# ScalarE's queue order, whole-row state copies and a halved last transfer in a kernel of two sequence layers

## The chip, the cores and the metric

The kernel runs on one core of one Trainium2 chip. The metric is the device time of one execution in microseconds; less is better. The kernel before takes 144.13 us, the median of three runs (144.0 to 144.6).

## The reference

Two independent layers on sequences of 2048 tokens with 448 features, their outputs side by side.

```
# A: a diagonal complex state space layer (448 states)
Lam_bar = exp(dt * Lam);  Bu = x @ B_bar.T
h[t] = Lam_bar * h[t-1] + Bu[t]
a = 2 * Re(h @ C.T) + x * Dskip

# B: attention with 16 heads of 28, each token sees 8 tokens, 2 apart
q, k, v = split(x @ wqkv)
logits[s, w] = q[s] . k[s - 2*w] * 28**-0.5      (w = 0..7)
b = (softmax_w(logits) weighted sum of v[s - 2*w]) @ wo

out = concat([a, b], axis=-1)
```

## The kernel before

Part B holds the sequence as 128 chunks (partitions) of 16 tokens. `proj_t` computes transposed q and k, `products` and `sums` form the logits in `lgs`, and `proj(j)` gives the values of token j of each chunk; its copy out of PSUM into `vd` is ACT's (ScalarE's) work at L163. The softmax is made in two halves of 8 tokens. The second half (`softmax(1)`) turns the logits with TensorE into two PSUM tiles `lt`, takes maxima on VectorE (L388, L389), exponentials on ACT (L391), sums over the 8 places with TensorE (`den`) and then the weights (L404, L405). The first half (`softmax(0)`) is turned by a DMA and kept in SBUF (`st`, with `self.low` a view of it); VectorE does its maxima (`low_turned`), ACT one exponential of 1024 per partition (L408, `expo_turned`), VectorE its sums (`norm_sums`, L417). The weighted sums of values run on VectorE for four tokens at a time: `pv` (L479, L482) and three times `pv_paired` (products L493, adds L497), where three of the adds are done by accumulating DMAs that GpSimd issues (L503). `tail` turns the sums with a DMA transpose on SyncE's queue (L524) into `oT`, and `wo_ps` matmuls (L533) give the output.

Part A holds the sequence as 512 blocks of 4 tokens. `level1_halves` (L137) and `level1` (L734, L738) compute the states within a block for the 7 groups m of 64 states; `keep` copies them into `h` (L745, and L747 for the fourth token), and `self.kept` is the last of the former so far. `scan(mh)` carries the states over the 128 chunks in 7 doubling rounds, each a few small matmuls (L779) and an ACT copy (L782) into `pbuf`. It runs for three sets `MH` of groups, of 4, 2 and 1. `ends(mh)` then gives the state before each block in `G`: an ACT copy of the chunk ends `hc` into every fourth column (L789), and for each m six matmuls (L798) into a PSUM tile `gt` of three parts of 128, which ACT copies into the other columns (L800). `correct(b, m)` multiplies a row of `G` (`co`, L805) and VectorE adds it to `h` (L806); `y` forms the output (L818 with the skip tiles `Dg`, L822), and ACT copies it out (L825).

What sets the order:

- TensorE's is mostly written out by hand: `chain` ties each matmul to the one before. `lanes` walks through steps of two half-height matmuls each; `weave` is a list of pairs (step, functions), and a function is called when its step is reached. Its `BEGIN` and `WEAVE` entries are the logits; (144, turn) turns the second half's logits, (163, prepare) emits its sums and `skip`, 170 and 178 start `pv`, (200, ...) emits the first half's exponential. `scan`, `level1` and `ends` are not in the chain; the compiler's scheduler places them by the order in which they are emitted and by its own costs.
- `vchain` does the same for VectorE, `gchain` for GpSimd.
- `cx.order(ins, after, "NoSync")` says that an instruction stands behind another on the same engine, without a wait of its own. Other orders on ACT are the scheduler's.
- At the end, products of the first half are made through `each`: from the fourth of these instructions on, each is followed by two `correct` steps on VectorE, and the `co` matmuls are set into TensorE's line of `y` and `wo` matmuls.
- `mats_behind` lets VectorE build matrices of powers (L702) behind a given instruction.

Of the kernel before, what the change touches and what calls it, by code (L numbers as in the profile page):

```python
# [11 lines left out]
ACT = mybir.ActivationFunctionType  # L12
ALU = mybir.AluOpType
AX = mybir.AxisListType
f32 = mybir.dt.float32
bf16 = mybir.dt.bfloat16
# [4 lines left out]
NCH = 128  # L21
KT = 4
KP = 112
KA = 128
NF = 512
PADK = 16
H = 16
DH = 28
W = 8
DIL = 2  # L30
HALO = (W - 1) * DIL
# [6 lines left out]
NST = 7  # L38
PAD = 64
MH = ((0, 4), (4, 6), (6, 7))  # L40
# [127 lines left out]
class PartB:  # L168
# [82 lines left out]
    def proj(self, j, eng):  # L251
        xv = self.xT[:].rearrange("f k (t j) -> f k j t", j=T)

        def alloc(odd):
            ps = self.cx.ps([NCH, D], f32, "v_ps")
            return ps[:], self.cx.halves(odd, lambda r, k: xv[r, k, j], lambda r, k: self.wn[r, k, 2 * D:])

        def done(ps):
            self.cx.ev(eng, self.vd[:, HALO + j], ps.rearrange("p (h d) -> p d h", h=H))

        return alloc, done

# [111 lines left out]
    def softmax(self, hf):  # L374

        nc, mm, V, cx, pool = self.nc, self.nc.tensor.matmul, self.nc.vector, self.cx, self.pool
        lv = self.lgs
        mx = pool.tile([NCH, 2, 4, H], bf16, name="mx", tag="mx")
        e = pool.tile([NCH, W, QH], bf16, name="e", tag="e")
        at = pool.tile([NCH, W, HJ, H], bf16, name=f"attn{hf}", tag=f"attn{hf}")  # L380
        lt = [None, None]

        def turn(i):
            lt[i] = cx.ps([NCH, 4, NCH], f32, f"lt{hf}{i}", "lg")
            out = [mm(lt[i][:, j, :], lhsT=lv[:, HJ * hf + 4 * i + j], rhs=cx.ident[:], start=(j == 0), stop=(j == 3),
                      skip_group_check=True).ins for j in range(4)]
            v = lt[i][:].rearrange("p j (w h) -> p j w h", w=W)
            cx.vchain(V.tensor_reduce(mx[:, i], v.rearrange("p j w h -> p j h w"), axis=AX.X, op=ALU.max).ins)  # L388
            self.maxima = V.tensor_tensor(v, v, mx[:, i].unsqueeze(2).to_broadcast([NCH, 4, W, H]), op=ALU.subtract).ins  # L389
            cx.vchain(self.maxima)  # L390
            nc.scalar.activation(e[:, :, 64 * i:64 * i + 64].rearrange("p w (j h) -> p j w h", h=H), v, ACT.Exp, scale=DH ** -0.5)  # L391
            return out

        def norm():
            den, out = cx.ps([NCH, QH], f32, "den", "lg"), []
            for w in range(W):
                out.append(mm(den[:], lhsT=cx.ident[:], rhs=e[:, w], start=(w == 0), stop=(w == W - 1)).ins)
            weights(den[:], lambda ins: None)
            return out

        def weights(den, each):
            rec = pool.tile([NCH, 1, QH], bf16, name="rec", tag="rec")
            with nc.allow_low_precision("softmax weights are bf16"):
                each(V.reciprocal(rec[:, 0], den).ins)  # L404
            each(V.tensor_tensor(at[:].rearrange("p w j h -> p w (j h)"), e[:], rec[:].to_broadcast([NCH, W, QH]), op=ALU.mult).ins)  # L405

        def expo_turned(after):
            cx.order(nc.scalar.activation(e[:].rearrange("p w (j h) -> p j w h", h=H), self.low, ACT.Exp, scale=DH ** -0.5).ins,  # L408
                     after, "NoSync")
            return []  # L410

        def norm_sums():
            src, n, c = e[:], W, W * QH
            for i in range(3):
                n //= 2
                dst = self.st[:, c:c + 2 * n * QH].bitcast(f32).rearrange("p (w q) -> p w q", q=QH)
                cx.vchain(V.tensor_tensor(dst, src[:, 0:n], src[:, n:2 * n], op=ALU.add).ins)  # L417
                src, c = dst, c + 2 * n * QH
            weights(src[:, 0], cx.vchain)
            return []  # L420

        return ([lambda: turn(0), lambda: turn(1), norm] if hf else [self.low_turned, expo_turned, norm_sums]), at

    def turn_first(self):

# [61 lines left out]
    def pv_paired(self, hf, at, jl0, each, last=False, between=lambda: None):  # L487

        nc, V, n, b = self.nc, self.nc.vector, 4, self.pvb

        def product(w, t_, c0=0, c1=n):
            off = HALO + HJ * hf + jl0 - DIL * w
            each(V.tensor_tensor(t_[:, c0:c1], at[:, w, jl0 + c0:jl0 + c1, :].unsqueeze(2).to_broadcast([NCH, c1 - c0, DH, H]),  # L493
                                 self.vd[:, off + c0:off + c1], op=ALU.mult).ins)

        def add(t_, u_, c0=0, c1=n):
            each(V.tensor_tensor(t_[:, c0:c1], t_[:, c0:c1], u_[:, c0:c1], op=ALU.add).ins)  # L497

        for w in range(0, 6, 2):
            t_, u_ = b[:, 1 + w], b[:, 2 + w]  # L500
            product(w, t_)
            product(w + 1, u_)
            self.cx.gchain(nc.gpsimd.dma_start(t_.rearrange("p j d h -> p (j d h)"), u_.rearrange("p j d h -> p (j d h)"),  # L503
                                               accum_op=ALU.add).ins)
        acc, u_ = b[:, 0], b[:, 2]
        product(6, acc)
        product(7, u_)
        add(acc, u_)
        add(acc, b[:, 1])
        add(acc, b[:, 3])  # L510
        between()
        for c0, c1 in ((0, 2), (2, 4)) if last else ((0, 4),):
            add(acc, b[:, 5], c0, c1)
        self.outs.append(self.tail(hf, jl0, acc, last))
# [28 lines left out]
class PartA:  # L543
# [137 lines left out]
    def skip(self):  # L681
        nc, ident = self.nc, self.cx.ident
        ptd = self.cx.ps([KA, KT], bf16, "pt_d", "lg")
        out = [nc.tensor.transpose(ptd[:], self.drow[:], ident[0:KT, 0:KT]).ins]
        dsk = self.pool.tile([KA, KT], f32, name="dsk")
        nc.scalar.copy(dsk[:], ptd[:])
        self.Dg = self.pool.tile([KA, KT, KA], bf16, name="Dg")
        for k in range(KT):
            nc.scalar.activation(self.Dg[:, k, :], ident[:], ACT.Copy, scale=dsk[:, k:k + 1])
        return out  # L690

    def mats_behind(self, keys, after):
        for i in keys:
# [90 lines left out]
    def ends(self, mh):  # L784
        nc, cx = self.nc, self.cx
        M, v = self.mats, self.h[3]
        hc, m0, m1 = self.pbuf[mh][NST % 2], *MH[mh]
        Gv = self.G[:, :, 1:1 + NF].rearrange("p m (c a) -> p m a c", a=4)
        nc.scalar.copy(Gv[:, m0:m1, 3], hc[:, :, PAD:PAD + NCH])  # L789
        for m in range(m0, m1):  # L790
            vm = v[:, m, :]
            hp = hc[:, m - m0, PAD - 1:PAD - 1 + NCH]
            ps = cx.ps([NCH, 3 * NCH], f32, "gt", "mm")
            mm = [(cx.ident[:], vm[:, 0:3 * NCH], 0, 3), (M[4][:, m, :], vm[:, 0:2 * NCH], 1, 3),
                  (M[8][:, m, :], vm[:, 0:NCH], 2, 3), (M[4][:, m, :], hp, 0, 1), (M[8][:, m, :], hp, 1, 2),
                  (M[12][:, m, :], hp, 2, 3)]
            for i, (l_, r_, c0, c1) in enumerate(mm):
                nc.tensor.matmul(ps[:, c0 * NCH:c1 * NCH], lhsT=l_, rhs=r_, start=(i == 0), stop=(i == 5),  # L798
                                 skip_group_check=True)
            nc.scalar.copy(Gv[:, m, 0:3], ps[:].rearrange("p (a c) -> p a c", a=3))  # L800

    def correct(self, b, m):
        nc, cx = self.nc, self.cx
# [27 lines left out]
def body(ctx: ExitStack, tc: tile.TileContext, A_x, A_Lre, A_Lim, A_Bre, A_Bim, A_Cre, A_Cim, A_logdt, A_Dskip,  # L831
         B_x, B_wqkv, B_wo, out):
    nc = tc.nc
# [3 lines left out]
    cx = Ctx(tc, pool, psum)  # L837
    b = PartB(cx, B_x, B_wqkv, B_wo, out_v[:, :, D:2 * D])
# [71 lines left out]
    qk, soft = b.qk(), {}  # L910
# [4 lines left out]
    def turn():  # L915
        a.mats_behind([5, 6, 7, 1], b.product)
        soft[1] = b.softmax(1)
        return soft[1][0][0]() + soft[1][0][1]()

    def prepare():  # L920
        a.mats_behind([8, 9], b.maxima)
        return soft[1][0][2]() + a.skip()

    def behind_values():
# [7 lines left out]
    def begin():  # L932
        soft[0] = fs, at0 = b.softmax(0)

        def put(*fs):
            return lambda after: [x for f in fs for x in ((f() if callable(f) else a.mats_behind([f], after)) or ())]

        soft["pv"] = b.pv(1, soft[1][1], 0, 4, between=[put(fs[0]), put(10), put(2)], each=cx.vchain)
        return more()

    def more():
        return next(soft["pv"]) + next(soft["pv"])

    weave += [(144, [turn]), (156, [behind_values]), (163, [prepare]), (170, [begin]), (178, [more]),
              (200, [lambda: soft[0][0][1](a.kept)])]
    weave.sort(key=lambda x: x[0])
    cx.lanes([b.proj_t(t0, t1, g, "A") for t0, t1, gs in ((256, 512, (0, 1, 2)), (0, 512, (3,)), (256, 512, (4, 5, 6)))
              for g in gs]
# [2 lines left out]
    at0, wo = soft[0][1], b.outs  # L951
    deque(soft["pv"], 0)
    a.alloc_scan()
    b.pv_paired(1, soft[1][1], 4, cx.vchain, between=soft[0][0][2])
    for mh in range(3):
        if mh:
            a.level1(mh)
# [65 lines left out]
```

## Time and profile before

| | |
|---|---|
| three runs, median | 144.13 us (144.0 to 144.6) |
| profiled execution, own time | 143.81 us |
| its span, first to last instruction | 142.0 us |
| granted TensorE clock, mean | 0.995 |
| busy in the span | TensorE 131.2, VectorE 121.9, ScalarE 89.4, GpSimd 17.9 us |

The profile is one execution. The 1.8 us between its own time and its span lie around the first and the last instruction. Names such as L163 are lines of the kernel; L163 is a helper, so the tile's name tells which copy it is. Matmuls are pipelined and their ends modelled, so that a busy TensorE need not be at its peak.

### The profile page before, as it was taken

How to read it: one execution, taken by the hardware profiler on the slowest of the kernel's cores; microseconds unless marked ns; L12 is line 12 of the kernel's file. 1: busy time of each engine (PE TensorE's matmuls, PEld its weight loads, DVE VectorE, ACT ScalarE, POOL GpSimd, SP SyncE). 2: the span in 40 equal slices, each digit the busy share in tenths (PEclk: the TensorE clock that was granted, in tenths of full speed). 3: DMA queues.
4: the chain of work that ended last, by engine and by line, in shares of the span. 5: the costliest groups of instructions: out<-in, count | busy, mean ns of one | idle time of the engine just before them, and what ended most of it. 6: DMA issues, size and time to landing. Idle time of an engine off the chain costs nothing.

```text
span 142.0 us, 3235 instructions
## 1 busy us (share of the span) xinstructions
PE 131.2 (92%) x1212; PEld 75.8 (53%) x1216; DVE 121.9 (86%) x158; ACT 89.4 (63%) x192; POOL 17.9 (13%) x113
## 2 busy tenths in 40 slices
PE   6899999999999978998999999979999999999990
PEld 2565535445666733555666456666455545555450
DVE  4689999999999976999999999974999999996300
ACT  2767596976694486556899968999552212354360
POOL 7301000000000000001201420030110001320000
PEclk9999999999999999999999999999999999999997
DMA  3999999999955999990004993099374118899482
GB/s 92 324 221 183 185 204 147 164 159 145 203 113 124 175 269 143 250 195 1 0 0 87 171 195 68 2 218 248 89 158 135 65 65 166 177 230 266 90 232 75
DMA packets 47150, 21.41 MB, mean 151 GB/s; under 512 B 38739, under 2 KB 45601, under 8 KB 47135
## 3 DMA queue, kind: packets, MB, share of 16 engines
q1 hardware_dynamic: 45365, 16.57, 57.1%
q0 software_dynamic: 1296, 4.13, 15.5%
q10 hardware_dynamic: 474, 0.52, 1.1%
q8 instruction: 9, 0.15, 0.4%
q14 instruction: 6, 0.05, 0.1%
HBM read 3.91 MB, written 3.67 MB: 53 GB/s over the span
## 4 chain that ended last, share of the span: by engine, by line
PE 54%; DVE 22%; ACT 15%; issue 4%; DMA 2%; POOL 0%; ACTq 0%; DVEq 0%
PE qk_ps L137 14%; PE y_ps L822 7%; DVE h L806 7%; PE l1h L137 6%; PE l L734 5%; PE lg L353 4%; PE wo_ps L533 4%; PE v_ps L137 3%; DVE pvb L497 3%; ACT h L745 2%; DVE pr L342 2%; ACT pbuf L782 2%; DMA oT<-pvb 2%; PE warm L73 2%; ACT h L747 2%
## 5 line engine op out<-in xcount | busy, mean ns | idle before, releaser
L493 DVE TENSOR_TENSOR pvb<-attn,vd 128x1792 bf16<-128x1792 bf16 x24 | 24.9, 1085 | 0.0
L137 PE MATMUL qk_ps<-xbT,wqkv_nat 64*128 64x512 bf16 (+1 forms) x168 | 21.4, 351 | 0.1
L825 ACT CAST ya<-y_ps 128x448 bf16<-128x448 f32 x16 | 8.5, 532 | 19.4 <-PE y_ps L822 17.7
L342 DVE TENSOR_TENSOR pr<-q,kd 128x3072 bf16<-128x3072 bf16 x11 | 19.0, 1752 | 0.4 <-ACT q L163 0.4
L822 PE MATMUL y_ps<-Ccat,h 128*128 128x448 bf16 x84 | 18.5, 352 | 0.0
L137 PE MATMUL l1h<-xaT,Bcat 64*128 64x512 bf16 x112 | 16.0, 376 | 0.8 <-ACT vd L163 0.7
L806 DVE TENSOR_TENSOR h<-co,h 128x512 bf16<-128x512 f32 x21 | 13.7, 684 | 2.7 <-PE co L805 2.7
L533 PE MATMUL wo_ps<-wo_p,oT 128*128 128x448 bf16 (+1 forms) x68 | 14.2, 341 | 0.5 <-DMA oT<-pvb 0.4
L497 DVE TENSOR_TENSOR pvb<-pvb 128x1792 bf16<-128x1792 bf16 (+1 forms) x13 | 13.1, 1016 | 1.5 <-DMA pvb<-pvb 1.3
L503 POOL DMA_DIRECT2D pvb<-pvb x9 | 7.8, 864 | 49.7 <-DVE pvb L493 49.7
L137 PEld LDWEIGHTS <-wqkv_nat 64*128 64x128 bf16 x168 | 9.1, 94 | 8.5 <-POOL spot L146 1.9
L163 ACT CAST kd<-qk_ps 128x512 bf16<-128x512 f32 (+4 forms) x26 | 10.4, 426 | 5.0 <-PE qk_ps L137 4.4
L734 PE MATMUL l<-xaT,Bcat 128*128 128x512 bf16 x45 | 12.6, 379 | 0.1
L137 PE MATMUL v_ps<-wqkv_nat,xbT 64*128 64x448 bf16 x112 | 12.5, 357 | 0.0
L146 POOL MEMSET spot<- 1x1 f32 x59 | 5.2, 88 | 57.2 <-PE qk_ps L137 24.9
L137 PEld LDWEIGHTS <-Bcat 64*128 64x128 bf16 x112 | 6.7, 94 | 7.7 <-issue 3.5
L163 ACT CAST q<-qk_ps 128x512 bf16<-128x512 f32 (+2 forms) x23 | 9.9, 461 | 1.4 <-PE qk_ps L137 1.3
L822 PEld LDWEIGHTS <-h 128*128 128x128 bf16 x84 | 7.4, 98 | 6.2 <-issue 0.9
L782 ACT CAST pbuf<-l 128x512 bf16<-128x512 f32 (+2 forms) x21 | 9.2, 437 | 1.0 <-PE l L779 0.8
L533 PEld LDWEIGHTS <-oT 128*128 128x128 bf16 x68 | 6.3, 97 | 6.4 <-DMA oT<-pvb 0.9
L137 PEld LDWEIGHTS <-xbT 64*128 64x128 bf16 x112 | 7.6, 144 | 3.7 <-POOL spot L146 0.9
L163 ACT CAST vd<-v_ps 128x448 bf16<-128x448 f32 x16 | 7.6, 534 | 2.8 <-PE v_ps L137 2.8
(140 smaller groups left out, 239.8 us busy)
## 6 DMA issues: line engine op xcount, KB each, us to landing
pvb<-pvb POOLq DMA_DIRECT2D x9, 448.0 KB, 5.0
out_dram<-ya SPq DMA_DIRECT2D x19, 112.0 KB, 1.8
out_dram<-yb SPq DMA_DIRECT2D x12, 112.0 KB, 3.0
vd<-vd SPq DMA_DIRECT2D x1, 784.0 KB
vd<-vd SPq DMA_DIRECT2D x1, 588.0 KB, 5.3
xn<-in_B_x_dram SPq DMA_DIRECT2D x2, 224.0 KB, 2.6
wqkv_nat<-in_B_wqkv_dram ACTq DMA_DIRECT2D x2, 224.0 KB, 4.4
wqkv_nat<-in_B_wqkv_dram SPq DMA_DIRECT2D x2, 224.0 KB, 4.0
```

What stands on the lines that cost most here:

```text
L137: ins = mm(g["ps"], lhsT=l_, rhs=r_, start=first, stop=not (g["left"][0] or g["left"][1]), skip_group_check=True).ins
L163: return self.nc.scalar.copy(out, in_).ins
L342: self.queued(V.tensor_tensor(pr, q[0][:, qu].unsqueeze(2).to_broadcast([KA, KT - 1, 4, n]), self.shifted(self.kT[:, 2 * i + qu], s), op=A ...
L493: each(V.tensor_tensor(t_[:, c0:c1], at[:, w, jl0 + c0:jl0 + c1, :].unsqueeze(2).to_broadcast([NCH, c1 - c0, DH, H]), self.vd[:, off + c0: ...
L497: each(V.tensor_tensor(t_[:, c0:c1], t_[:, c0:c1], u_[:, c0:c1], op=ALU.add).ins)
L503: self.cx.gchain(nc.gpsimd.dma_start(t_.rearrange("p j d h -> p (j d h)"), u_.rearrange("p j d h -> p (j d h)"), accum_op=ALU.add).ins)
L533: done.append(nc.tensor.matmul(ps[:], lhsT=oT[:, 7 * i + 3 * odd + k, :], rhs=self.wo_p[:, odd, k, c:c + n], start=(k == 0), stop=(k == KT ...
L734: nc.tensor.matmul(ps[:], lhsT=self.Bcat[:, m, k, :], rhs=self.xT[:, b, k, :], start=(k == 0), stop=(b == 0 and k == KT - 1))
L782: nc.scalar.copy(dst[:, :, PAD:], ps[:])
L806: cx.vchain(nc.vector.tensor_tensor(h, ps[:], h, op=ALU.add).ins)
L822: out.append(nc.tensor.matmul(ps[:], lhsT=self.state(m, r, b), rhs=self.C[:, m, :], start=False, stop=(m == NM - 1), skip_group_check=True ...
L825: nc.scalar.copy(ya, ps[:])
```

## The change

- The second half's two exponentials are no longer emitted in `turn` but at steps 151 and 155, each behind the last `vd` copy emitted by then (`self.vcopied`).
- The first half's exponential becomes two of 512 per partition, at steps 200 and 206, each behind `a.kept` of that moment.
- The four skip tiles `Dg` move out of `skip` to steps 182 (two) and 187 (two), each behind `a.kept`.
- Matrix 10 is built with matrices 8 and 9, behind the maxima, and no longer between the products of `pv`.
- `ends` has no copy of `hc`: a seventh matmul with the identity puts it into a fourth part of `gt`, and one ACT copy per m writes a whole row of 512 of `G`, reading PSUM in steps of 128 floats.
- The last of the accumulating DMAs moves tokens 2 and 3 only; VectorE adds tokens 0 and 1.

```diff
@@ proj
-            self.cx.ev(eng, self.vd[:, HALO + j], ps.rearrange("p (h d) -> p d h", h=H))
+            self.vcopied = self.cx.ev(eng, self.vd[:, HALO + j], ps.rearrange("p (h d) -> p d h", h=H))
@@ softmax
-            nc.scalar.activation(e[:, :, 64 * i:64 * i + 64].rearrange("p w (j h) -> p j w h", h=H), v, ACT.Exp, scale=DH ** -0.5)
+            lt[i] = v
             return out
+        def expo(i, src, after):
+            cx.order(nc.scalar.activation(e[:, :, 64 * i:64 * i + 64].rearrange("p w (j h) -> p j w h", h=H), src, ACT.Exp,
+                                          scale=DH ** -0.5).ins, after, "NoSync")
+            return []
...
-        def expo_turned(after):
-            cx.order(nc.scalar.activation(e[:].rearrange("p w (j h) -> p j w h", h=H), self.low, ACT.Exp, scale=DH ** -0.5).ins,
-                     after, "NoSync")
-            return []
...
-        return ([lambda: turn(0), lambda: turn(1), norm] if hf else [self.low_turned, expo_turned, norm_sums]), at
+        if hf:
+            return [lambda: turn(0), lambda: turn(1), norm, lambda i: expo(i, lt[i], self.vcopied)], at
+        return [self.low_turned, norm_sums, lambda i, after: expo(i, self.low[:, 4 * i:4 * i + 4], after)], at
@@ pv_paired
-            self.cx.gchain(nc.gpsimd.dma_start(t_.rearrange("p j d h -> p (j d h)"), u_.rearrange("p j d h -> p (j d h)"),
+            c0 = 2 if last and w == 4 else 0
+            self.cx.gchain(nc.gpsimd.dma_start(t_[:, c0:].rearrange("p j d h -> p (j d h)"), u_[:, c0:].rearrange("p j d h -> p (j d h)"),
                                                accum_op=ALU.add).ins)
+            if c0:
+                add(t_, u_, 0, c0)
@@ skip
-        self.Dg = self.pool.tile([KA, KT, KA], bf16, name="Dg")
-        for k in range(KT):
-            nc.scalar.activation(self.Dg[:, k, :], ident[:], ACT.Copy, scale=dsk[:, k:k + 1])
+        self.dsk, self.Dg = dsk, self.pool.tile([KA, KT, KA], bf16, name="Dg")
         return out
+
+    def skip_mats(self, ks):
+        for k in ks:
+            ins = self.nc.scalar.activation(self.Dg[:, k, :], self.cx.ident[:], ACT.Copy, scale=self.dsk[:, k:k + 1]).ins
+            self.cx.order(ins, self.kept, "NoSync")
+        return ()
@@ ends
-        Gv = self.G[:, :, 1:1 + NF].rearrange("p m (c a) -> p m a c", a=4)
-        nc.scalar.copy(Gv[:, m0:m1, 3], hc[:, :, PAD:PAD + NCH])
...
-            ps = cx.ps([NCH, 3 * NCH], f32, "gt", "mm")
+            ps = cx.ps([NCH, NF], f32, "gt", "mm")
...
-                  (M[12][:, m, :], hp, 2, 3)]
+                  (M[12][:, m, :], hp, 2, 3), (cx.ident[:], hc[:, m - MH[mh][0], PAD:PAD + NCH], 3, 4)]
...
-            nc.scalar.copy(Gv[:, m, 0:3], ps[:].rearrange("p (a c) -> p a c", a=3))
+            nc.scalar.copy(self.G[:, m, 1:1 + NF].rearrange("p (c a) -> p c a", a=4),
+                           ps[:].rearrange("p (a c) -> p c a", a=4))
@@ body
-        a.mats_behind([8, 9], b.maxima)
+        a.mats_behind([8, 9, 10], b.maxima)
...
-        soft["pv"] = b.pv(1, soft[1][1], 0, 4, between=[put(fs[0]), put(10), put(2)], each=cx.vchain)
+        soft["pv"] = b.pv(1, soft[1][1], 0, 4, between=[put(fs[0]), put(2)], each=cx.vchain)
...
-              (200, [lambda: soft[0][0][1](a.kept)])]
+              (151, [lambda: soft[1][0][3](0)]), (155, [lambda: soft[1][0][3](1)]), (182, [lambda: a.skip_mats((0, 1))]),
+              (187, [lambda: a.skip_mats((2, 3))]), (200, [lambda: soft[0][0][2](0, a.kept)]),
+              (206, [lambda: soft[0][0][2](1, a.kept)])]
...
-    b.pv_paired(1, soft[1][1], 4, cx.vchain, between=soft[0][0][2])
+    b.pv_paired(1, soft[1][1], 4, cx.vchain, between=soft[0][0][1])
```

More of the change, by code (lines that the diff above doesn't have):

```diff
@@ L786, in ends @@
         M, v = self.mats, self.h[3]
-        hc, m0, m1 = self.pbuf[mh][NST % 2], *MH[mh]
-        Gv = self.G[:, :, 1:1 + NF].rearrange("p m (c a) -> p m a c", a=4)
-        nc.scalar.copy(Gv[:, m0:m1, 3], hc[:, :, PAD:PAD + NCH])
-        for m in range(m0, m1):
+        hc = self.pbuf[mh][NST % 2]
+        for m in range(*MH[mh]):
             vm = v[:, m, :]
-            hp = hc[:, m - m0, PAD - 1:PAD - 1 + NCH]
-            ps = cx.ps([NCH, 3 * NCH], f32, "gt", "mm")
+            hp = hc[:, m - MH[mh][0], PAD - 1:PAD - 1 + NCH]
+            ps = cx.ps([NCH, NF], f32, "gt", "mm")
             mm = [(cx.ident[:], vm[:, 0:3 * NCH], 0, 3), (M[4][:, m, :], vm[:, 0:2 * NCH], 1, 3),
                   (M[8][:, m, :], vm[:, 0:NCH], 2, 3), (M[4][:, m, :], hp, 0, 1), (M[8][:, m, :], hp, 1, 2),
-                  (M[12][:, m, :], hp, 2, 3)]
+                  (M[12][:, m, :], hp, 2, 3), (cx.ident[:], hc[:, m - MH[mh][0], PAD:PAD + NCH], 3, 4)]
             for i, (l_, r_, c0, c1) in enumerate(mm):
-                nc.tensor.matmul(ps[:, c0 * NCH:c1 * NCH], lhsT=l_, rhs=r_, start=(i == 0), stop=(i == 5),
+                nc.tensor.matmul(ps[:, c0 * NCH:c1 * NCH], lhsT=l_, rhs=r_, start=(i == 0), stop=(i == 6),
                                  skip_group_check=True)
-            nc.scalar.copy(Gv[:, m, 0:3], ps[:].rearrange("p (a c) -> p a c", a=3))
+            nc.scalar.copy(self.G[:, m, 1:1 + NF].rearrange("p (c a) -> p c a", a=4),
+                           ps[:].rearrange("p (a c) -> p c a", a=4))
     def correct(self, b, m):
```

## The prediction

> **What bounds the kernel now.** First the page's totals, then the waits of TensorE and VectorE, because TensorE is busy 92% of the span and a change can only win where it stands still or where its order is held up.
>
> ```profile
> span 142.0 us, 3235 instructions
> PE 131.2 (92%) x1212; PEld 75.8 (53%) x1216; DVE 121.9 (86%) x158; ACT 89.4 (63%) x192; POOL 17.9 (13%) x113
> ...
> PE l1h L137 <- ACT h L745: 1.2, 2, 0.7
> PE l1h L137 <- ACT vd L163: 0.7, 1, 0.7
> PE l L779 <- ACT pbuf L782: 0.7, 2, 0.4
> PE l L769 <- ACT h L747: 0.6, 1, 0.6
> PE wo_ps L533 <- DMA oT<-pvb: 0.4, 1, 0.4
> ...
> DVE h L806 <- PE co L805: 2.7, 1, 2.7
> DVE rec L404 <- PE den L397: 1.7, 1, 1.7
> ```
>
> The columns are total us, times, longest us. TensorE's waits after the start are for ScalarE (ACT), an engine busy 63%: ACT is not short of time, its queue has the wrong thing in front. The timeline of ACT shows what:
>
> ```profile
> 47.44 0.54 ACT L163 CAST vd<-v_ps 128x448 bf16<-128x448 f32 x1
> 50.04 0.60 ACT L391 ACTIVATE e<-lt 128x512 bf16<-128x512 f32 x1 [2.07 <-DVE lt L389]
> 50.53 0.53 ACT L163 CAST vd<-v_ps 128x448 bf16<-128x448 f32 x1
> 51.37 0.60 ACT L391 ACTIVATE e<-lt 128x512 bf16<-128x512 f32 x1 [0.31 <-DVE lt L389]
> 51.87 1.40 ACT L163 CAST vd<-v_ps 128x448 bf16<-128x448 f32 x3
> 54.38 0.16 ACT L686 CAST dsk<-pt_d 128x4 f32<-128x4 bf16 x1 [1.11 <-PE pt_d L684]
> 54.63 1.28 ACT L689 ACTIVATE Dg<-ident,dsk 128x128 bf16<-128x128 bf16 x4
> 55.81 2.02 ACT L745 CAST h<-l1h 128x512 bf16<-128x512 f32 x4
> ...
> 64.21 1.07 ACT L408 ACTIVATE e<-st 128x1024 bf16<-128x1024 f32 x1
> ...
> 80.15 1.35 ACT L789 COPY G<-pbuf 128x512 bf16<-128x512 bf16 x1
> ```
>
> (Start, us, engine, line; in brackets the idle time before and its releaser.) Each exponential, skip tile or G copy here stands ahead of a copy that TensorE soon needs. The end, from the same view of VectorE:
>
> ```profile
> 126.70 3.34 DVE L497 TENSOR_TENSOR pvb<-pvb 128x1792 bf16<-128x1792 bf16 x3
> 131.38 1.16 DVE L497 TENSOR_TENSOR pvb<-pvb 128x896 bf16<-128x896 bf16 x2 [1.33 <-DMA pvb<-pvb]
> ```
>
> **Which engine sets the end.** From 97.73, when the first `co` is ready, to 130.05 VectorE has no idle time but small gaps. In the correction phase the `co` matmuls come in pairs 2.2 us apart from 106.39 (106.39, 108.49, 110.69, 112.89, 115.09), exactly a 1.00 product and two 0.60 corrections on VectorE, against some 1.95 for the pairs before (104.44 to 106.39). So VectorE paces TensorE there, and TensorE's remaining line runs without a hole from the last `co` (118.51) until 134.67. The end thus follows the moment of the first `co` one for one, and the sum is the holes of TensorE ahead of it, plus the last one, 0.44.
>
> **The change, part by part.**
>
> *Second half's exponentials.* ACT stood 2.07 us for the first and 0.31 for the second while finished value copies lay behind; TensorE then lacked a PSUM buffer for 0.75 at 52.45. With two of those four copies ahead of the first exponential and the others around the second, copies run from about 49.4, the first exponential at 50.5 at the latest (its input is ready at 49.95), and the second ends between 51.97 (as now) and 52.65 (four copies of 0.53 and two exponentials of 0.53 from 49.4). The `den` matmuls, now at 53.61, would want it at 53.61 - 0.75 = 52.86. Gain 0.75; bounds 0.2 to 0.75. Queued behind the exponentials are `dsk` and the first `h` copies, not due before 53.
>
> *Skip tiles.* Four, 1.28 in all, sit ahead of the first four `h` copies, and TensorE waited 0.73 at 56.91 for them. Removed: 0.73. Put back as two pairs of 0.59 each (four at a pitch of 0.295) behind given `h` copies at steps 182 and 187. TensorE does a step in 0.213 from 56.91 (step 171 or 172), so these are near 59.1 and 60.2. ACT is idle 1.54 before 59.37, which hides the first pair; the second may delay two `h` copies. The same place one round later shows the slack: the exponential's 0.95 there cost TensorE 0.47, so 0.48 is free. Cost 0 to 0.11; without that cover, 0.59 each. `Dg` is first read at 97.95.
>
> *First half's exponential in two.* 1.07 becomes two of 0.60 (the L391 rows, same size), 0.53 each in the queue. One part between the pairs of copies costs 0.53 - 0.48 = 0.05, the other lies behind the second pair, in front of 1.54 of idle time. Of 0.47, 0.42 is won; with the skip pair above I take 0.35, bounds 0.25 to 0.47. Its reader, L417, starts at 86.87.
>
> *Matrix 10* moves 0.60 of VectorE into its 1.74 idle before L404 (now 54.27, then 53.52; the matrices end at 53.13): free, and VectorE is later earlier by 0.75 + 0.60 = 1.35. Its four products then end at 94.96 - 1.35 = 93.6, a limit on how early corrections can start: 4.1 ahead of 97.73.
>
> *Ends.* Out go three strided copies of `hc` (1.35, 0.82, 0.59); seven copies of 384 become copies of 512 that write whole rows; seven identity matmuls of 128 columns come in, at 0.055 (four 128-column skip matmuls in 0.20 to 0.22 at L818), 0.39 in all. What a new G copy costs is the largest unknown:
>
> ```profile
> L825 ACT CAST ya<-y_ps 128x448 bf16<-128x448 f32 x16 | 8.5, 532 | 19.4 <-PE y_ps L822 17.7 <-PE y_ps L818 1.7
> L163 ACT CAST vd<-v_ps 128x448 bf16<-128x448 f32 x16 | 7.6, 534 | 2.8 <-PE v_ps L137 2.8
> L800 ACT CAST G<-gt 128x384 bf16<-128x384 f32 x7 | 7.0, 1116 | 0.0
> L747 ACT CAST h<-l 128x512 bf16<-128x512 f32 x3 | 1.8, 619 | 0.0
> ```
>
> (Groups by form: busy us, mean ns of one.) L825 reads PSUM in order, the `vd` copies read it in steps of 28 floats, both write in order: 532 and 534 ns. L800 reads in order and writes every fourth element: 1116 ns for fewer. So the stepped write is the price, and a new copy should be near L747, stepped read and row written, 0.55 to 0.62. The other end is L800's rate, 1116 x 512/384 = 1490 ns. I take 0.60, nearest in size, type and steps.
>
> [...]
>
> At 80.15 the 1.35 copy delays `h` copies for the second scan: TensorE's 0.59 at 81.97 goes. From 89.35 to 95.72 the last scan's chain of small ACT copies has two G copies at a pitch of 0.93 and 0.66 of a `hc` copy in it; at 0.53 and 0 that is 0.80 + 0.66 = 1.46 less on the chain. TensorE cannot use it all: its idle there is 0.68 (90 to 95), and it does the 0.39 of new matmuls: 0.29 at the least, 1.1 if half of the excess counts as hidden behind its modelled busy time. I take 0.5. G waits after the first `co` (0.3 and 0.3) count nothing, as VectorE paces.
>
> *Last transfer.* VectorE gets one more add of 896, 0.58 (half of the last row above). It starts no wait if halves are kept apart, and they are: the first transpose on SP goes at 132.06, between the two half adds. VectorE's full adds would end at 130.05 - 2.92 + 0.58 = 127.71; the first half add follows with no DMA in it, ends at 128.26, and its transpose lands 3.06 later (132.06 to 135.12) at 131.32, while TensorE gets there at 134.67 - 2.92 = 131.75. So the 0.44 goes, with 0.43 of margin. The second half's transfer, issued at 124.96 - 2.92 = 122.04, takes at most the 6.4 of the whole one (landing at 128.4): no loss over 0.15.
>
> **Sum:** 0.75 + 0.73 + 0.35 + 0.59 + 0.50 + 0.44 = 3.36. The profiled run took 143.81 (span 142.0): 140.45 there, span 138.6. It is 0.32 under the median of 144.13, so 140.8. With the better ends, 4.2 off: 139.9; with the worse (0.20, 0.62, 0.25, 0.59, 0.29, 0.1), 2.05 off: 142.1.
>
> **Rivals.**
>
> *The extra add waits for the transfer* (slower). If the add of tokens 0 and 1 is held until the transfer on the same tile lands, VectorE stands at 121.73 until 122.04 plus 3.2 to 6.4, some 5.1; the half add ends near 133.4, the transpose at 136.4 instead of 131.75: 140.8 + 4.7 = 145.5. It decides from a wait of 3.8 on. The staggered transposes speak against it. Chance 0.07.
>
> *Whole rows are no cheaper.* At 1490 ns, pitch 1.40, the seven take 9.8 on ACT. The chain of the last scan grows 2 x 0.47 - 0.66 = 0.28 and TensorE 0.39, so 0.67 lost for the 0.50 won; later rows come 1.40 apart while VectorE takes two per 2.2, about 1.0 more. 140.8 + 2.2 = 143.0. [...]
>
> *The exponentials go too far back.* One more copy ahead moves `den` 0.5 late, and the waits for `h` stay in part: 141.5 to 142.5. For it: the slack is only 0.2 to 0.9. Chance 0.08, inside the range.
>
> *A new order in the ends.* The ends' matmuls and copies are not in the hand-written chain, so fewer and longer copies can be placed anew, ahead of the last scan's small copies; each such swap costs 0.3 to 0.5, and from seven on it eats the 3.36: 142 to 145. Chance 0.07.
>
> **Chances.** The forecast has the remaining 0.72. Under 0.5%, 0.7 us, this kernel's measurement cannot tell from no change. Faster: 0.72 + 0.08 + 0.04 of the rows that are no cheaper and 0.01 of the new order, 0.85; same 0.02 + 0.02 of these two, 0.04; slower 0.07 of the held add and 0.04 of the new order, 0.11. The range 139.9 to 143.1 leaves out the held add, most of the new order and a little on the low side.
>
> **What would show it.** Right: no wait of `l1h` for `vd` or `h` over 0.2; `Dg` near 57 to 60; G rows of 0.6; no `hc` copies; the first `co` near 94.8; no wait of `wo_ps` for `oT`. Wrong: DVE idle after 121 (held add), G rows over 1 us, `den` released by a late `e`, or a first `co` after 96.

## The result, and the profile after

The kernel after takes 140.0 us (median of 4 runs, 139.85 to 140.02) against 144.37 us for the kernel before (median of 4 runs, 144.0 to 144.6): a ratio of 0.9697, 95% interval 0.9671 to 0.9724. That is 4.37 us less; the forecast was 140.8 us, or 3.36 us off. Its profiled execution took 139.97, with a span of 138.2. One run in all the experiments below, 142.93 us in whole_transfer, was slow at a lower mean clock (0.986) and is left out of its ratio.

First the page's totals, then the waits of TensorE (after the start) and of VectorE (its start and end left out), to be held against those of before:

```profile
span 138.2 us, 3245 instructions
PE 131.0 (95%) x1219; PEld 76.2 (55%) x1223; DVE 122.4 (89%) x159; ACT 85.2 (62%) x190; POOL 18.0 (13%) x113
...
PE den L402 <- ACT e L395: 0.2, 1, 0.2
PE l L788 <- ACT pbuf L791: 0.2, 1, 0.2
...
DVE h L814 <- PE co L813: 0.6, 1, 0.6
DVE pvb L495 <- DMA pvb<-pvb: 0.4, 1, 0.4
```

The waits of `l1h` for `vd` and `h`, of the second scan for `h`, of `y_ps` for G and of `wo_ps` for `oT` are gone. Two small ones have come: `den` waits 0.17 for the second exponential, and a product of VectorE waits 0.4 for an accumulating transfer. The same stretch of ACT's timeline:

```profile
50.12 0.97 ACT L163 CAST vd<-v_ps 128x448 bf16<-128x448 f32 x2 [1.71 <-PE v_ps L137]
50.97 0.61 ACT L395 ACTIVATE e<-lt 128x512 bf16<-128x512 f32 x1
51.46 0.99 ACT L163 CAST vd<-v_ps 128x448 bf16<-128x448 f32 x2
52.30 0.65 ACT L395 ACTIVATE e<-lt 128x512 bf16<-128x512 f32 x1
...
57.74 1.07 ACT L754 CAST h<-l1h 128x512 bf16<-128x512 f32 x2 [1.62 <-PE l1h L137]
58.70 0.70 ACT L697 ACTIVATE Dg<-ident,dsk 128x128 bf16<-128x128 bf16 x2
59.30 1.07 ACT L754 CAST h<-l1h 128x512 bf16<-128x512 f32 x2
60.24 0.71 ACT L697 ACTIVATE Dg<-ident,dsk 128x128 bf16<-128x128 bf16 x2
```

Two value copies, an exponential, two copies, an exponential: the order that the prediction laid out. The skip tiles stand between and behind the pairs of `h` copies; the first pair does not fall into the 1.62 of idle time, as forecast, but behind it. The tail of VectorE:

```profile
121.49 0.62 DVE L499 TENSOR_TENSOR pvb<-pvb 128x896 bf16<-128x896 bf16 x1
122.03 2.08 DVE L495 TENSOR_TENSOR pvb<-attn,vd 128x1792 bf16<-128x1792 bf16 x2
124.15 4.54 DVE L499 TENSOR_TENSOR pvb<-pvb 128x1792 bf16<-128x1792 bf16 x5
```

The extra add (first row) starts without a wait, at 121.49, even before GpSimd's issue of the transfer of the tile's other half shows in its timeline (121.75), and the half adds at the end follow without the 1.33 of before: the slower rival, the held add, did not come.

**Marks.** The profiled executions are compared by marks of TensorE: first `lt` matmul, first `den`, first `l1h` matmul that reads `h`, first matmul of the first and of the second scan, first `co`, first matmul of the last `wo`, end of the span. All work ahead of `lt` is the same in all kernels, yet `lt` comes at 47.74 before, 48.18 after and 47.93 to 48.85 in the others. Where the first loads land is part of this: in the latest (pace), TensorE first waits 0.47 for `wqkv_nat` and 0.66 for `xn`, and the profile before lists neither wait. The stretches behind `lt` repeat within 0.05 us wherever their code is the same (two exceptions, a longer transfer in skip176 and a lower clock in corr4x3, are told below), so they show more than the whole times can. The last two columns take in the span, which the profile gives to a tenth, and are good to some 0.1.

| | lt | lt to den | to h | to scan 1 | to scan 2 | to co | to last wo | to end | lt to end |
|---|---|---|---|---|---|---|---|---|---|
| before | 47.74 | 5.87 | 3.30 | 12.09 | 12.97 | 15.34 | 37.81 | 6.88 | 94.26 |
| after | 48.18 | 4.82 | 2.38 | 11.84 | 12.23 | 14.90 | 36.95 | 6.90 | 90.02 |
| exp2_alone | 48.02 | 4.82 | 3.28 | 12.10 | 12.97 | 15.34 | 37.86 | 6.91 | 93.28 |
| skip_alone | 48.06 | 5.86 | 2.40 | 12.26 | 12.97 | 15.37 | 37.84 | 6.84 | 93.54 |
| exp1_alone | 47.95 | 5.86 | 3.29 | 11.67 | 12.98 | 15.34 | 37.81 | 6.90 | 93.85 |
| ends_alone | 47.96 | 5.86 | 3.30 | 12.09 | 12.23 | 14.91 | 37.56 | 6.89 | 92.84 |
| transfer_alone | 48.01 | 5.86 | 3.30 | 12.09 | 12.98 | 15.34 | 37.20 | 6.92 | 93.69 |
| whole_transfer | 48.27 | 4.82 | 2.39 | 11.83 | 12.23 | 14.94 | 37.57 | 6.85 | 90.63 |
| stepped_rows | 47.93 | 4.82 | 2.39 | 11.83 | 12.23 | 16.09 | 38.01 | 6.90 | 92.27 |
| pace | 48.85 | 4.82 | 2.38 | 11.84 | 12.23 | 14.91 | 37.13 | 6.84 | 90.15 |
| skip176 | 48.25 | 4.82 | 2.38 | 11.56 | 12.24 | 14.90 | 37.51 | 6.94 | 90.35 |
| corr4x3 | 48.08 | 4.82 | 2.38 | 11.83 | 12.24 | 14.89 | 38.22 | 8.44 | 92.82 |
| corr5x3 | 48.00 | 4.82 | 2.39 | 11.83 | 12.23 | 14.93 | 37.42 | 6.88 | 90.50 |
| both | 48.17 | 4.82 | 2.38 | 11.56 | 12.22 | 14.90 | 37.74 | 6.91 | 90.53 |

### The profile page after: what moved, and what is told of

It is laid out like the page before. It is cut to its first block, busy times and chain, and to the rows that moved or that the text cites. A ratio compares the mean times of both kernels' runs of the same rounds, so it can differ in the third digit from the quotient of the medians.

```text
span 138.2 us, 3245 instructions
## 1 busy us (share of the span) xinstructions
PE 131.0 (95%) x1219; PEld 76.2 (55%) x1223; DVE 122.4 (89%) x159; ACT 85.2 (62%) x190; POOL 18.0 (13%) x113
## 4 chain that ended last, share of the span: by engine, by line
PE 67%; DVE 15%; ACT 12%; issue 2%; POOL 0%; DVEq 0%; ACTq 0%
PE qk_ps L137 14%; PE y_ps L830 9%; PE v_ps L137 8%; DVE h L814 7%; PE l L743 7%; PE lg L353 6%; PE l1h L137 5%; PE wo_ps L538 4%; ACT h L754 3%; DVE pvb L495 3%; DVE pvb L499 3%; PE gt L805 2%; PE warm L73 2%; PE l L788 2%; ACT pbuf L791 2%
## 5 line engine op out<-in xcount | busy, mean ns | idle before, releaser
L137 PE MATMUL l1h<-xaT,Bcat 64*128 64x512 bf16 x112 | 15.4, 376 | 0.0
L499 DVE TENSOR_TENSOR pvb<-pvb 128x1792 bf16<-128x1792 bf16 (+1 forms) x14 | 13.8, 991 | 0.3
```

Of the source, the lines that this page charges most:

```text
L137: ins = mm(g["ps"], lhsT=l_, rhs=r_, start=first, stop=not (g["left"][0] or g["left"][1]), skip_group_check=True).ins
```

## The experiments

Ratios are to runs of the kernel before on the same chip, with 95% intervals. The kernel after was timed in a session of its own, and the median of the kernel before was 144.14 to 144.37 in the four sessions, so a difference of some 0.3 us from the kernel after is not shown by the times alone.

**The parts alone.** Each is the kernel before with one group of the change's lines.

```diff
# exp2_alone
-            nc.scalar.activation(e[...], v, ACT.Exp, scale=DH ** -0.5)      # in turn(i)
+            lt[i] = v
+    (151, [lambda: soft[1][0][3](0)]), (155, [lambda: soft[1][0][3](1)])    # expo(i, lt[i], self.vcopied)
```

> The kernel before with one part of the change: the second half's two exponentials behind the value copies of steps 151 and 155. Theory (the end follows TensorE's holes ahead of the first co): 0.75 to 1.05 us faster, den 4.8 instead of 5.9 after the first lt matmul, and every later mark of TensorE up to the first co earlier by the same. Rival (the weights are what counts, and they are no earlier): end unchanged, within 0.3 us.

143.16 us, ratio 0.9943 (0.9919 to 0.9966). `lt` to `den` falls from 5.87 to 4.82 as expected, all other stretches stay: the theory holds, and 1.05 is more than the row's 0.75.

```diff
# skip_alone
-        for k in range(KT):
-            nc.scalar.activation(self.Dg[:, k, :], ident[:], ACT.Copy, scale=dsk[:, k:k + 1])
+    (182, [lambda: a.skip_mats((0, 1))]), (187, [lambda: a.skip_mats((2, 3))])
```

> The kernel before with one part of the change: the four skip tiles in two pairs at steps 182 and 187. Theory: 0.6 to 0.9 us faster; the wait of l1h for h at the first b=1 matmul is gone (0.73 in the profile before) and the second pair costs 0.1 or less. Rival (the tiles only change places): the pairs delay h copies of the next round by what they saved, gain under 0.3 us.

143.38 us, ratio 0.9939 (0.9923 to 0.9955). The hole before the first `h` matmul shrinks by 0.90, the next stretch grows by 0.17: a small part does only change places, more than the 0.1 that the theory allowed. By the starts of the single matmuls the cost is one new hole, at 61.35: a step of two matmuls starts 0.50 after the one before, where 0.216 is usual, so 0.28 is lost. Against it, 0.11 goes that was still lost right behind the old hole. In the kernel after, with the same lines, the hole is at 60.42, and the `h` copies that end just ahead of it (59.30 + 1.07 = 60.37) are the two behind the first pair of tiles; the second pair costs nothing that shows.

```diff
# exp1_alone
-              (200, [lambda: soft[0][0][1](a.kept)])]
+              (200, [lambda: soft[0][0][2](0, a.kept)]), (206, [lambda: soft[0][0][2](1, a.kept)])]
```

> The kernel before with one part of the change: the first half's exponential in two parts at steps 200 and 206. Theory (each hole of TensorE is longer than its row of the waits by what the last matmul's modelled length exceeds its pitch, some 0.16): the hole at 66.30 is 0.47 + 0.16, one part of 0.53 in the same place leaves 0.05, so 0.4 to 0.6 us faster. Rival (the row as it stands): 0.35 to 0.42. Rival (no hole on the path): within 0.2 of before.

144.03 us, ratio 0.9975 (0.9956 to 0.9995); 12.09 to 11.67 by the marks, 0.42. That is the number of the row as it stands, and the low end of the theory, but TensorE's timeline bears out the theory's longer hole. Before, and then in this run:

```profile
65.22 0.61 PE L137 MATMUL l1h<-xaT,Bcat 64*128 64x512 bf16 x4
66.30 0.37 PE L137 MATMUL l1h<-h,mat 64*128 64x512 bf16 x1 [0.47 <-ACT h L745]
```

```profile
65.41 0.61 PE L137 MATMUL l1h<-xaT,Bcat 64*128 64x512 bf16 x4
66.07 0.37 PE L137 MATMUL l1h<-h,mat 64*128 64x512 bf16 x1
```

Four such matmuls take 0.43 from start to start where nothing holds them. Here they take 1.08 before and 0.66 in this run, so the hole was 0.65, not 0.47, and 0.23 of it is left, not 0.05. Both ends are longer than their rows by nearly the same, and the difference hides it.

```diff
# ends_alone
-            nc.scalar.copy(Gv[:, m, 0:3], ps[:].rearrange("p (a c) -> p a c", a=3))
+            nc.scalar.copy(self.G[:, m, 1:1 + NF].rearrange("p (c a) -> p c a", a=4),
+                           ps[:].rearrange("p (a c) -> p c a", a=4))
# with the identity matmul, without the copies of hc
```

> The kernel before with one part of the change: the identity matmuls and whole rows of G. Theory: G copies of 0.55 to 0.62 us, 0.6 us gained at the second scan's start, 0.5 to 0.9 ahead of the first co, together 1.1 to 1.6 us faster. Rival (reading PSUM in steps of 512 bytes is slow): G copies of 1.1 us or more, at most 0.6 us faster.

142.7 us, ratio 0.9901 (0.9872 to 0.9929). From the first scan to `co` 28.31 becomes 27.14, and 0.25 more goes behind the first `co`: 1.42 together. G copies by these lines take 593 ns in the kernel after; the rival, a slow read of PSUM in steps, is out.

```diff
# transfer_alone
+            c0 = 2 if last and w == 4 else 0
...
+            if c0:
+                add(t_, u_, 0, c0)
```

> The kernel before with one part of the change: the last accumulating transfer for two tokens, the other two added by VectorE. Theory: TensorE's 0.44 us of waiting for the last oT goes and nothing else moves, 0.3 to 0.5 us faster. Rivals: the extra add is held until the transfer lands, 2 to 5 us slower; or the add of 0.55 eats what the transfer saves, within 0.2 us of before.

143.51 us, ratio 0.9945 (0.9924 to 0.9965). Only the stretch to the last `wo` changes, by 0.61. The wait row had said 0.44, and the theory 0.3 to 0.5.

The five ratios leave out 0.0057 + 0.0061 + 0.0025 + 0.0099 + 0.0055 = 0.0297, each good to 0.002 to 0.003; the whole change leaves out 0.0303. By the marks 1.05 + 0.73 + 0.42 + 1.42 + 0.61 = 4.23, the whole 4.24. The parts add up; matrix 10, in none of them, has no share that shows.

**Undoing the transfer** in the kernel after (its function as before).

```diff
# whole_transfer
-            c0 = 2 if last and w == 4 else 0
-            if c0:
-                add(t_, u_, 0, c0)
```

> The kernel after with the last part undone: the last transfer whole again and no extra add. Theory: VectorE's last half adds wait again for the transfer, the first transpose is late, TensorE waits 0.4 to 0.5 by the row and 0.6 by the pitch: 0.5 to 0.8 us slower than the kernel after. Rival (the tail was won elsewhere): within 0.2 of it.

140.71 us, ratio 0.9748 (0.9720 to 0.9775), 0.71 over the kernel after; the marks give 37.57 for 36.95, so 0.62. Theory right.

**Which side of the copy costs.**

```diff
# stepped_rows: the kernel after, same bytes, other order
-            nc.scalar.copy(self.G[:, m, 1:1 + NF].rearrange("p (c a) -> p c a", a=4),
-                           ps[:].rearrange("p (a c) -> p c a", a=4))
+            nc.scalar.copy(self.G[:, m, 1:1 + NF].rearrange("p (c a) -> p a c", a=4),
+                           ps[:].rearrange("p (a c) -> p a c", a=4))
```

> The kernel after, but the copy of a row of G reads PSUM in order and writes every fourth element, four sweeps over the row (the same bytes, the other order). Theory (the stepped write is the price): 1.4 to 1.5 us a copy, the first co about 0.3 to 1 later and corrections waiting for rows, 1 to 3 us slower than the kernel after. Rival (a copy's time hangs on its length, or on PSUM's steps): near 0.6 us a copy or faster, end unchanged.

142.28 us, ratio 0.9863 (0.9832 to 0.9895). The group of G copies, by form, in this kernel and in the kernel after:

```profile
L807 ACT CAST G<-gt 128x512 bf16<-128x512 f32 x7 | 8.5, 1434 | 0.1
```

```profile
L807 ACT CAST G<-gt 128x512 bf16<-128x512 f32 x7 | 4.1, 593 | 0.1
```

One size, one source, one target: 1434 ns with the step on the write, 593 with the step on the PSUM read. Both sides change together, so the run compares the two orders and not each side by itself. The first `co` comes 1.19 later (0.3 to 1 was expected) and the rows that follow cost 1.06 more. The prediction's price for a copy that is no cheaper was 2.2; it is 2.25 here.

**Who paces the correction phase.**

```diff
# pace: the kernel after; ten co matmuls run twice, right behind each other
+        if (b * NM + m) % 2:
+            self.twice[id(ins)] = nc.tensor.matmul(ps[:], lhsT=self.mats[b + 1][:, m, :], rhs=self.G[:, m, 0:NF], start=True, stop=True).ins
```

> The kernel after with ten of the 21 co matmuls done twice (the second overwrites the first with the same), one in each pair: 10 x 0.216 = 2.2 us more for TensorE in the correction phase and nothing more for VectorE. Theory (VectorE paces there, TensorE has some 0.25 us free in each pair): end within 0.4 us of the kernel after. Rival (TensorE is the bound there too): 1.8 to 2.2 us slower.

140.68 us, ratio 0.9747 (0.9717 to 0.9777): 0.68 over the kernel after, above the theory's 0.4 and far under the rival's 1.8. The marks tell the two apart: from the first `co` to the last `wo` the 2.2 us of matmuls cost 0.18; from the start of VectorE's first correction, 95.45, to that of its last, 117.44, it is 21.99 us, against 21.97 in the kernel after. The rest of this profile's difference is its late `lt` (48.85, 0.67 later). All four runs lie above the kernel after (140.45 to 140.89); whether the other three started late too is not shown.

**Can the rest be had?** Four versions aim at what is left: VectorE's 0.56 before the first `co`, TensorE's free 0.25 a pair, and the 0.17 of the skip tiles.

```diff
# skip176
-              (182, [lambda: a.skip_mats((0, 1))]),
-              (187, [lambda: a.skip_mats((2, 3))]),
+              (176, [lambda: a.skip_mats((0, 1, 2, 3))]),
# corr4x3
-        for n in range(2 * (len(steps) >= 4)):
+        for n in range(3 * (len(steps) >= 4)):
# corr5x3
+        for n in range(3 * (len(steps) >= 5)):
# both: skip176 and corr5x3
```

> The kernel after with all four skip tiles at step 176, behind the last h copy of the first round, in ACT's 1.6 us of idle time before the second round's copies. Theory (the pairs at 182 and 187 delay h copies and cost 0.17 between the first h matmul and the first scan): that stretch of TensorE 11.84 -> about 11.67, end 0.1 to 0.2 us earlier than the kernel after. Rival (the 0.17 is the half exponential's): stretch unchanged.

139.92 us (139.5 to 140.32), ratio 0.9696 (0.9674 to 0.9718): not to be told from the kernel after. The stretch to the first scan does fall, by 0.28. But in the profiled run the gain is lost on VectorE:

```profile
82.64 1.09 DVE L495 TENSOR_TENSOR pvb<-attn,vd 128x1792 bf16<-128x1792 bf16 x1 [1.35 <-DMA pvb<-pvb]
```

This product writes a buffer that an accumulating DMA, issued at 76.59, still reads. In the kernel before there was no wait, in the kernel after 0.41, here 1.35. The length of the transfer itself decides this, not how early VectorE comes: it landed 4.6 us after its issue before, 5.0 in the kernel after and 6.0 here, while in the run `both`, with the same code up to here, the wait was 0.4. exp1_alone, where VectorE is no earlier than before, has a wait of 0.4 too. Here VectorE, not `co`, starts the corrections (95.14), and the last `wo` is 0.36 later than after. This profiled execution is the slowest of the five; whether the 0.28 reaches the end when the transfer lands sooner is not shown.

> The kernel after with three corrections instead of two behind each step of VectorE from the fourth on: VectorE's total is the same, TensorE is no longer held in pairs. Theory (TensorE has 0.25 us free in each pair, but the end needs VectorE's last sums and their transpose as well, which land just as TensorE arrives): TensorE comes 1 to 2.5 us earlier to the last wo and waits there for oT; end within 0.3 us of the kernel after. Rival (TensorE's pacing alone sets the end): 1 to 2.5 us faster.

140.98 us, ratio 0.9799 (0.9760 to 0.9838), 1.0 over the kernel after, where within 0.3 was expected. The profiled execution is the slowest of six (142.71; the others took 140.81 to 141.50). TensorE did run ahead and waited, as expected, but VectorE was not where it was: now TensorE's `co`, 0.975 apart, holds it (its waits for `co` are 1.1 in all), its last full adds start at 125.37 instead of 124.15, and after the long wait something else follows (below).

> As the run with three corrections, but from the fifth step on, so that VectorE makes one more product while it waits 0.56 us for the first co. Theory (both engines bound the tail): VectorE's last sums and the oT transpose come 0.5 earlier, end 0.3 to 0.6 us earlier than the kernel after. Rival (corrections pushed back hold TensorE): same or slower.

140.28 us, ratio 0.9733 (0.9713 to 0.9754): 0.28 over the kernel after (0.48 by the marks) where 0.3 to 0.6 less was expected. The reason is the same: the five products come first, then VectorE follows TensorE's spacing, and its last full adds start at 124.52, 0.55 later than in the kernel after when both are counted from `lt`. TensorE waits 1.82 for `oT`.

> Three corrections from the fifth step on and all skip tiles at step 176. Theory: the first co comes 0.17 earlier, and VectorE, which already has its five products until 0.4 us after that, does not follow: same as the run with five and three within 0.2 us. Rival (gains add): 0.15 to 0.2 us faster than that run.

140.42 us, ratio 0.9748 (0.9723 to 0.9774). The earlier `co` brings nothing, as the theory said. None of the four is shown to beat the kernel after.

## Why the prediction was right

The direction, the order of the steps and the place of each gain were as laid out. The time lies in the range, but at its very edge: 140.0 for a lower bound of 139.9. That bound was set too low by two slips. The better ends, as the terms state them, add up to 4.08 and not 4.2, which gives 140.05. Among them, the 1.1 for the ends is the whole excess of 1.46 - 0.39; with half of the excess, as the words have it, it is 0.68, and the bound some 140.5, above the measured time. So the range holds it by luck. Most terms came out larger than forecast, for one reason in the main: wait rows were taken for the whole of the holes. Term by term, from the marks:

- *Second half's exponentials:* 0.75 forecast, 1.05 measured. The term was mis-sized because the row of waits counts only the time in which TensorE is wholly idle by the modelled ends of its matmuls, and leaves out short waits. TensorE's timeline, before and then after:

```profile
50.24 0.38 PE L137 MATMUL l1h<-xaT,Bcat 64*128 64x512 bf16 x1
...
50.44 1.26 PE L137 MATMUL l1h<-xaT,Bcat 64*128 64x512 bf16 x7
52.45 1.24 PE L137 MATMUL l1h<-xaT,Bcat 64*128 64x512 bf16 x9 [0.75 <-ACT vd L163]
53.61 0.62 PE L397 MATMUL den<-e,ident 128*128 128x128 bf16 x8
```

```profile
50.68 0.38 PE L137 MATMUL l1h<-xaT,Bcat 64*128 64x512 bf16 x1
...
50.87 1.95 PE L137 MATMUL l1h<-xaT,Bcat 64*128 64x512 bf16 x16
53.00 0.61 PE L402 MATMUL den<-e,ident 128*128 128x128 bf16 x8 [0.17 <-ACT e L395]
```

  The same 17 matmuls take 3.37 to `den` before and 2.32 after, 0.17 of it the new wait. Of the 1.22 that was lost before, 0.75 was in the row. The starts of the single matmuls place most of the rest: 0.17 at the same hole, which reaches from the modelled end of a matmul and not from where the next could have started, and 0.24 at a smaller hole at 51.11, of which only 0.06 counts as idle and no row is listed. No run varied these alone.
- *Skip tiles:* 0.73 forecast, 0.90 measured at the hole. The row starts at the modelled end of the last matmul, 376 ns after its start, where the next could start after 213; the 0.163 between is lost too. The pairs cost 0.17 net, over the bound of 0.11: a hole of 0.28, less the 0.11 that went with the old hole. The first pair was taken to fall into idle time, falls behind the first two `h` copies instead and makes the hole. With all four tiles at step 176 the stretch is shorter by just this 0.28. The slack at this place was also read too large, 0.48, as 0.95 of exponential less a row of 0.47. By the starts some 0.3 is free there: the whole exponential takes 0.96 of ACT and costs 0.65, the half one takes 0.53 and costs 0.23, the pair of tiles takes 0.60 and costs 0.28.
- *First half's exponential:* 0.42, as worked out, though neither the 0.47 that was there nor the 0.05 that was to be left is the whole of its hole (0.65 and 0.23); the two errors cancel. With the skip pairs 0.25 instead of the 0.35 taken, the lower bound.
- *Ends, up to the first `co`:* 0.59 + 0.50 = 1.09 forecast, 1.18 measured (28.31 to 27.13): 0.74 up to the second scan and 0.44 from there. G copies take 593 ns, 600 was taken. The 0.50 was a guess between bounds whose upper one came from a misreading: by the starts of ACT's instructions the two G copies in the last scan's chain have pitches of 0.76 and 0.78, not 0.93, and the `hc` copy one of 0.51, not 0.66, so the chain loses some 1.0 and not 1.46. That the 0.50 came out near is in part luck. The first `co` is ready for VectorE at 94.78, as asked ("near 94.8"), in an execution that started 0.44 later; counted from `lt` it comes 3.4 earlier, where 2.92 was forecast.
- *G waits behind the first `co`:* nothing forecast, 0.25 measured. VectorE's corrections had small gaps there, which were passed over.
- *Last transfer:* 0.44 forecast, 0.61 measured; again the modelled end, 352 ns against a pitch of 190.

Sum 1.05 + 0.90 - 0.17 + 0.42 + 1.18 + 0.25 + 0.61 = 4.24 from `lt` to the end; the spans differ by 3.80 only, because the profiled execution of before happened to start 0.44 earlier. This would also explain why it was 0.32 to 0.56 under the medians of its kernel; no trace of the others shows it.

The claim that VectorE sets the pace behind the first `co` held (pace: 2.2 us of added matmuls cost 0.18). The claim that the end follows the first `co` one for one holds for the gains of the parts, each of which reached the end whole; it stops there: past this point VectorE's sums, TensorE's line and the accumulating transfers end within a few tenths of each other (by the marks corr5x3 ends 0.48 later than the kernel after, skip176 0.33).

Of the rivals, the held add and the new order in the ends did not occur, and `den` was 0.17 late by the exponential, where the rival of exponentials too far back had 0.5. Rows that are no cheaper (0.04 + 0.02 of the chances) did not occur either: a copy took 593 ns with the write in a row and 1434 with the write in steps.

## What to carry to other kernels

Where an engine that is not busy holds up one that is, look at what stands first in its queue; moving a long, not yet needed instruction behind a short, awaited one gave back 1.05 of 1.22 us at the second half's exponentials and the whole 0.90 at the skip tiles (0.17 net went again where they were put), and several such holes add up as long as the same engine is late after each (4.23 for the parts, 4.24 for the whole). Read a hole from the starts of the matmuls on both sides, not from the wait row: where matmuls overlap, the row leaves out their modelled length less their pitch (0.376 less 0.213 here), and waits too short to be listed are left out whole (0.24 at 51.11 in the kernel before). Of the two orders of a transposing copy on ScalarE that were measured here, the one that writes in a row and reads PSUM in steps took 593 ns, the other 1434 (128x512 from f32 to bf16); for other sizes and types, measure both.

## What was not expected of the hardware

In corr4x3 TensorE stood idle for the last `oT` and then ran the same 20 matmuls in 4.84 us instead of some 3.22. The row of corr4x3, and that of corr5x3:

```profile
132.46 4.84 PE L538 MATMUL wo_ps<-wo_p,oT 128*128 128x448 bf16 x20 [2.25 <-DMA oT<-pvb]
```

```profile
131.62 3.23 PE L538 MATMUL wo_ps<-wo_p,oT 128*128 128x448 bf16 x20 [1.82 <-DMA oT<-pvb]
```

The busy times by stretch show why; the number behind the engines' busy times is the granted clock of TensorE (corr4x3):

```profile
131.00:132.00 1.00, 0.00 (x0) 0.00 (x0) 0.00 (x0) 0.00 (x0) 0.00 (x0) 1.00 0.85 158
133.00:134.00 1.00, 1.00 (x5) 0.37 (x3) 0.00 (x0) 0.00 (x0) 0.00 (x0) 0.50 0.83 252
```

After 2.25 us of idle time the granted clock was 0.50 for some 3.4 us; after 1.82 us, in corr5x3, it stayed at 1.00. Of the six executions of corr4x3 this is the slowest. The mean clocks of the others, 0.995 to 1.0 against 0.988, leave no room for such a stretch, which takes 0.012 off the mean. No single length of idle time fits all the profiles: behind the last matmul of a profiled execution the clock fell 2.1 us later in the kernel before (138.35 to 140.49) and 3.5 us later in the kernel after (134.52 to 138.02). What decides the moment is not shown, and what the shortest harmful gap is was not tried.
